# Moving two VectorE casts of chunk 4 behind the masks of chunk 3 in a fused attention and FFN kernel

## The chip, the cores and the metric

The kernel runs on one core of a Trainium2 chip. The metric is the device time of one execution in microseconds; lower is better. TensorE (PE in the profile, with its weight loads as PEld), VectorE (DVE), ScalarE (ACT) and GpSimd (POOL) work beside each other, each through its own instructions in order, and SyncE (SP) issues most of the DMAs in order too. An engine that meets an instruction whose inputs aren't ready waits there with all that stands behind it.

## What is computed

Attention over 4 batches of 8 heads, 768 positions, head size 64, where a query sees the first 4 positions (the sinks) and a window of 128 positions back. Its output, 3072 tokens of 512 numbers, goes through a feed-forward layer that takes the largest of three products:

```python
scores = scale * np.matmul(q, k.transpose(0, 1, 3, 2))
keep = is_sink | in_window
scores = np.where(keep, scores, -1000000000.0)
a = np.exp(scores - np.max(scores, axis=-1, keepdims=True))
a = a / (np.sum(a, axis=-1, keepdims=True) + 1e-09)
x = np.matmul(a, v)                    # then (B*S, H*D)
h = np.maximum(np.maximum(x @ w1, x @ w2), x @ w3)
out = h @ w_out
```

## The kernel before

The tokens are cut into 12 chunks of 256, three to a batch, so that chunks 0, 3, 6 and 9 begin a batch and have no sinks to look back to. A chunk's heads go in four pairs, 0 to 3. For each chunk `load` (lines 93 to 110) brings Q, K and V as float32 into `q_raw`, `k_raw` and `v_raw`, two buffers each; `cast_qk` (112 to 119) turns one half (two pairs) of Q or K into bf16 (`q_bf`, `k_bf`) on the engine that is named in the call; and the halves together are turned to have the head dimension on the partitions, into `qT` and `kT`. Chunks 0 to 3 are turned on TensorE (`turn`). From chunk 4 on a transposing DMA does it (`turn_dma`, 177 to 189), one for Q and, up to chunk 5, two for K. All of them are issued by SP.

Then, pair by pair: `score` (314 to 337) multiplies keys by queries into PSUM (line 331), `expo` (392 to 399) takes the exponential on ScalarE into `e_sb` (line 398), `mask` (401 to 406) multiplies `e_sb` by zeros and ones on VectorE (line 406), and `av` (460 to 476) multiplies it by V (line 471). `av` ends in `norm` (478 to 486), which divides on VectorE by the row sums into `x_sb` (lines 481 and 484). When all four pairs of a chunk are normed, `xpose_dma` (501 to 505) turns `x_sb` into `xT` with one more transposing DMA from SP (line 503). The FFN of a chunk reads `xT`: `ffn_h` (511 to 530) is called nine times a chunk, for three weights and three column blocks, with 8 matmuls each (line 524). Its maximum is a ScalarE copy for the first weight (line 536) and a VectorE maximum for the others (line 540). `ffn_y` multiplies by the output weight (line 553).

There is no scheduler: the kernel is written under `manual_schedule`, and the order of the calls from line 639 on is the order of the instructions on each engine. The FFN of one chunk fills TensorE while the attention of the next is prepared. Around the change the FFN of chunk 2 runs beside the attention of chunk 3, and Q, K and V of chunks 4 to 6 are loaded, cast and turned.

Eight PSUM banks are handed on in the order in which they are given back (`bank` and `give`, 57 to 65). `ffn_h(2, 1, 1)` takes the bank that `ffn_h(2, 0, 1)` has used, `ffn_h(2, 0, 2)` that of pair 0's `norm`.

What stands on the queues between lines 810 and 857, where the change lies:

- VectorE: mask of pair 1, then in the kernel before the cast of half 1 of Q of chunk 4 and of half 0 of K of chunk 4, then the masks of pairs 0 and 3, the maximum for `ffn_h(2, 0, 1)`, the norms of pairs 0 and 1, mask of pair 2, norm of pair 3, two more maxima, a cast for chunk 5, and the norm of pair 2, the last of chunk 3.
- TensorE: scores of pairs 1, 2, 0 and 3, three `ffn_h` of chunk 2 (24 matmuls), `av` of pairs 0 and 1, one `ffn_h`, `av` of pair 3, two `ffn_h`, `av` of pair 2, three `ffn_h`, then sinks and scores of chunk 4 and `ffn_y` of chunk 2, and then `ffn_h(3, 0, 0)`, the first that reads `xT` of chunk 3.
- SP: `turn_dma` of Q of chunk 4, `turn_dma` of its K (two transfers), the load of V of chunk 5 (behind a one-element write of POOL, line 619), `xpose_dma(3)`, the loads of K, V and Q of chunk 6.
- POOL: casts of V of chunk 3 and K of chunk 4, two casts of V of chunk 4, the one-element write, `sink_k` (line 283, two small copies), and from the landing of V of chunk 5 on an unbroken row of casts.

Of the kernel before, what the change touches and what calls it, by code (L numbers as in the profile page):

```python
# [16 lines left out]
def kernel(  # L17
# [13 lines left out]
    nc = tc.nc  # L31
# [17 lines left out]
    with tc.manual_schedule():  # L49
# [7 lines left out]
        def bank(shape, dtype, name):  # L57
            j = free.pop(0)
            x = psum.tile(shape, dtype, tag=f"b{j}", name=name)
            home[id(x)] = x, j  # L60
            return x
# [18 lines left out]
        def keys(ci):  # L80

            return (kT[ci % RING].rearrange("q n p i r -> q (n p i r)")
                    .rearrange("q (p n h c) -> q p n h c", p=NP, n=2, h=2))
# [28 lines left out]
        def cast_qk(ci, w, g, eng):  # L112

            if (ci, w) not in bfs:
                bfs[ci, w] = raw.tile([128, NP, 2, 2, D], BF16, tag=w + "_bf", name=w + "_bf")
            x, y = bfs[ci, w], raws[ci, w]
            f = eng.copy if eng is nc.scalar else eng.tensor_copy
            f(x[:, 2 * g:2 * g + 2].rearrange("q p i a d -> q p a i d"),  # L118
              y[:, 4 * g:4 * g + 4].rearrange("q (p a) i d -> q p a i d", a=2))

        def cast_v(ci, n, i, eng):
            if ci < NEW:
                eng.tensor_copy(  # L123
                    vb[ci % RING][64 * i:64 * i + 64, n, :, 0:D],
                    raws[ci, "v"][64 * n:64 * n + 64, :, i])
                return
            for h in range(2):
                x, y = 64 * h + 32 * i, 64 * n + 32 * h
                eng.tensor_copy(  # L129
                    vb[ci % RING][x:x + 32, n, :, 0:D], raws[ci, "v"][y:y + 32, :, i])  # L130
# [46 lines left out]
        def turn_dma(ci, w):  # L177
            if ci >= NCH:
                return
            if w == "k" and ci < NEW:  # L180
                for n in range(2):
                    nc.sync.dma_start_transpose(
                        out=kT[ci % RING][:, n].rearrange("q p i r -> q (p i) r"),
                        in_=bfs[ci, w][64 * n:64 * n + 64].rearrange("q p i a d -> q (p i a d)"))
                return
            dst = (qT[ci % RING].rearrange("q p i n r -> q (p i) (n r)") if w == "q" else
                   keys(ci).rearrange("q p n h c -> q (p n) (h c)"))
            nc.sync.dma_start_transpose(
                out=dst, in_=bfs[ci, w].rearrange("s p i a d -> s (p i a d)"))
# [124 lines left out]
        def score(ci, pairs):  # L314
            if ci >= NEW:
                return score4(ci, pairs)
            b, c = divmod(ci, CPB)
            kc, qc = kT[ci % RING], qT[ci % RING]
            lo = 0 if c else 1
            for p in pairs:  # L320
                add = (ci, p) in sts
                if not add:
                    sts[ci, p] = [bank([128, 4, 128], F32, "st") for a in range(2)]
                st = sts[ci, p]
                for s, x, n, q0, q1 in ((0, kT[(ci - 1) % RING], 1, 0, 1), (1, kc, 0, 0, 2),
                                        (3, kc, 1, 1, 2)):
                    if s < lo:
                        continue
                    for a in range(2):
                        hp = slice(64 * a, 64 * a + 64)  # L330
                        nc.tensor.matmul(  # L331
                            st[a][:, s:s + q1 - q0].rearrange("q n (i r) -> q n i r", i=2),
                            lhsT=x[hp, n, p].rearrange("q i r -> q (i r)"),
                            rhs=qc[hp, p, :, q0:q1].rearrange("q i n r -> q n i r"),
                            start=not add, stop=True, skip_group_check=add)
                e = work.tile([128, 2, 4, 128], BF16, tag="e", bufs=2 * NP, name="e_sb")
                es[ci, p] = e, st
# [39 lines left out]
        def mask4(ci, p):  # L377
            e = es[ci, p][0]
            if ci % CPB == 0:
                nc.vector.tensor_mul(e[:, :, 1:], e[:, :, 1:], msk0[1])  # L380
                return
            x = work.tile([128, 2, 4, 128], BF16, tag="e", bufs=2 * NP, name="e_sb")


            y = e.rearrange("q a (t j) r -> q (a t) (j r)", t=2)
            (ps, pn), (gs, gn), (cs, cn) = y.ap
            y = bass.AP(tensor=y.tensor, offset=y.offset,
                        ap=[[ps, pn], [gs, gn], [64 * cs, 2], [cs, 128]])
            nc.vector.tensor_mul(x.rearrange("q a (t s) c -> q (a t) s c", t=2), y, msk2)  # L389
            es[ci, p] = x, None  # L390

        def expo(ci, p):
            if ci >= NEW:
                return expo4(ci, p)
            lo = 0 if ci % CPB else 1
            e, st = es[ci, p]
            for a in range(2):
                nc.scalar.activation(e[:, a, lo:], st[a][:, lo:], AF.Exp, scale=scale)  # L398
                give(st[a])

        def mask(ci, p, eng=None):
            if ci >= NEW:
                return mask4(ci, p)
            lo = 0 if ci % CPB else 1
            e = es[ci, p][0]
            (eng or nc.vector).tensor_mul(e[:, :, lo:], e[:, :, lo:], msk0[0] if lo else msk)  # L406
# [104 lines left out]
        def ffn_h(ci, fp, wi, cuts=1, eng=nc.scalar, then=True):  # L511
            if ci not in hs:
                hs[ci] = work.tile([128, FB, 256], BF16, tag="h", bufs=3, name="h_sb")
            hp = bank([128, 2, 256], F32, "h_ps")
            for f in range(2):
                c0 = (2 * fp + f) * 128
                for ds in range(DS):
                    x = xTs[ci][:, ds]
                    if ci < NEW:
                        x = x.rearrange("q t (i r) -> q i t r", i=2)  # L520
                    else:
                        x = (x.rearrange("q t c -> q (t c)")
                             .rearrange("q (j i r) -> q i j r", i=2, r=32))
                    nc.tensor.matmul(  # L524
                        hp[:, f].rearrange("q (i t r) -> q i t r", i=2, r=x.shape[3]),
                        lhsT=w_sb[wi][:, ds, c0:c0 + 128], rhs=x,
                        start=(ds == 0), stop=(ds == DS - 1))
            maxima[ci, fp, wi] = hp
            if then:
                ffn_max(ci, fp, wi, cuts, eng)  # L530

        def ffn_max(ci, fp, wi, cuts=1, eng=nc.scalar):
            hp = maxima.pop((ci, fp, wi))
            dst = hs[ci][:, 2 * fp:2 * fp + 2]
            if wi == 0:
                (nc.scalar.copy if eng is nc.scalar else eng.tensor_copy)(dst, hp)  # L536
            else:
                for f in range(cuts):
                    x = slice(2 * f // cuts, 2 * (f + 1) // cuts)
                    nc.vector.tensor_max(dst[:, x], dst[:, x], hp[:, x])  # L540
            give(hp)
# [273 lines left out]
        cast_v(3, 1, 1, nc.gpsimd)  # L815
        score(3, (0,))
        expo(3, 0)
        cast_qk(4, 'q', 1, nc.vector)
        turn_dma(4, 'q')
        score(3, (3,))  # L820
        cast_qk(4, 'k', 0, nc.vector)
        cast_v(3, 1, 0, nc.gpsimd)
        expo(3, 3)
        mask(3, 0)
        ffn_h(2, 0, 0)
        mask(3, 3)
        ffn_h(2, 1, 0)
        ffn_h(2, 0, 1)
        av_open(3)
# [171 lines left out]
```

## Time and profile before

| | us |
|---|---|
| median of 3 runs | 176.84 (176.4 to 177.53) |
| the profiled execution | 176.56 |
| its span, first to last instruction | 174.8 |
| TensorE busy in it | 168.0 |
| VectorE busy | 126.9 |
| GpSimd busy | 113.1 |
| ScalarE busy | 87.8 |

The profile is of one execution. Times in its rows count from the start of the span. A row of the timeline holds the start, the duration, the engine, the line of the kernel, the operation and what it writes and reads (partitions by elements), how many like it were merged, and in brackets how long the engine sat idle before it and what ended that. SPq is the issue of a DMA by SP, not the transfer: the time from the start of the issue to the landing of the data stands in the view of the DMA issues. The PE clock that was granted is full in every slice of the page.

### The profile page before, as it was taken

The numbers are of one execution on the slowest core, as the hardware profiler recorded it, in microseconds if no ns is written. First come the engines' busy times: TensorE is split into PE (matmuls) and PEld (weight loads), VectorE is DVE, ScalarE is ACT, GpSimd is POOL, SyncE is SP. The second block draws the span as 40 slices with busy tenths as digits, with TensorE's granted clock in tenths as the row PEclk, the third lists the DMA queues.
The fourth block names the chain that finished last, engine by engine and source line by source line (L and its number), as shares of the span: only waits on it lengthen the run. The fifth ranks groups of instructions, "written<-read, shape, count | busy, mean of one in ns | idle before, by whom it ended". The sixth has DMA issues, their size and how long they took to land.

```text
span 174.8 us, 5427 instructions
## 1 busy us (share of the span) xinstructions
PE 168.0 (96%) x2229; PEld 129.4 (74%) x2229; DVE 126.9 (73%) x263; ACT 87.8 (50%) x182; POOL 113.1 (65%) x195
## 2 busy tenths in 40 slices
PE   7988999999989999999999999999999999999992
PEld 2445989756877688697797797797797796896871
DVE  2397665578799768886996886976887776776451
ACT  3688636666852742925827617717636516510210
POOL 6489880076962999999999999999999900000000
PEclk9999999999999999999999999999999999999999
DMA  4999999999977992899999989999999119117303
GB/s 144 292 288 197 237 263 204 270 274 290 285 138 173 200 284 42 192 294 227 247 204 256 270 172 223 267 181 216 244 213 265 32 25 358 44 32 268 124 2 120
DMA packets 70201, 35.22 MB, mean 201 GB/s; under 512 B 27552, under 2 KB 68000, under 8 KB 70176
## 3 DMA queue, kind: packets, MB, share of 16 engines
q1 hardware_dynamic: 64160, 30.55, 73.4%
q0 software_dynamic: 5872, 4.20, 14.5%
q8 instruction: 17, 0.28, 0.6%
q10 hardware_dynamic: 144, 0.13, 0.2%
q14 instruction: 8, 0.07, 0.1%
HBM read 25.17 MB, written 6.29 MB: 180 GB/s over the span
## 4 chain that ended last, share of the span: by engine, by line
PE 70%; DMA 15%; POOL 10%; issue 2%; SPq 1%; DVE 0%; POOLq 0%
PE h_ps L524 44%; PE y_ps L577 11%; PE o L471 5%; DMA w<-in_moe_w_dram 4%; DMA q_raw<-in_q_dram 4%; PE y_ps L553 4%; POOL vb L123 4%; DMA k_raw<-in_k_dram 4%; PE st L357 3%; DMA v_raw<-in_v_dram 3%; POOL w L292 2%; PE st L331 1%; POOL q_raw L107 1%; SPq L107 1%; PE o L453 1%
## 5 line engine op out<-in xcount | busy, mean ns | idle before, releaser
L524 PE MATMUL h_ps<-xT,w 128*128 128x256 bf16 x864 | 101.0, 273 | 0.1
L524 PEld LDWEIGHTS <-w 128*128 128x128 bf16 x864 | 82.0, 98 | 10.1 <-issue 0.3
L540 DVE TENSOR_TENSOR h_sb<-h_sb,h_ps 128x512 bf16<-128x512 bf16 (+1 forms) x74 | 49.1, 671 | 22.1 <-PE h_ps L524 20.7
L536 ACT CAST h_sb<-h_ps 128x512 bf16<-128x512 f32 x36 | 21.1, 592 | 46.5 <-PE h_ps L524 45.5
L129 POOL CAST vb<-v_raw 32x512 bf16<-32x512 f32 x48 | 34.6, 721 | 2.3
L90 POOL CAST k_bf<-k_raw 32x512 bf16<-32x512 f32 x48 | 31.6, 658 | 2.2
L398 ACT ACTIVATE e_sb<-st 128x512 bf16<-128x512 f32 (+1 forms) x48 | 23.3, 583 | 2.3 <-PE st L331 2.3
L484 DVE TENSOR_TENSOR x_sb<-o,rc 128x256 bf16<-128x256 f32 x48 | 20.4, 425 | 1.6
L577 PE MATMUL y_ps<-wo,h_sb 64*64 64x512 bf16 (+1 forms) x312 | 21.1, 377 | 0.0
L123 POOL CAST vb<-v_raw 64x512 bf16<-64x512 f32 x19 | 12.2, 645 | 10.5 <-DMA v_raw<-in_v_dram 9.8
L471 PE MATMUL o<-vb,e_sb 128*128 128x65 bf16 x352 | 16.4, 194 | 1.2 <-POOL ks L283 0.6
L471 PEld LDWEIGHTS <-e_sb 128*128 128x128 bf16 x352 | 14.3, 97 | 3.8 <-DVE e_sb L406 0.9
L389 DVE TENSOR_TENSOR e_sb<-e_part,msk 128x1024 bf16<-128x1024 bf16 x16 | 12.9, 815 | 3.4 <-ACT e_part L374 3.1
L406 DVE TENSOR_TENSOR e_sb<-e_sb,msk 128x1024 bf16<-128x1024 bf16 (+1 forms) x16 | 13.0, 836 | 2.9 <-ACT e_sb L398 2.9
L577 PEld LDWEIGHTS <-h_sb 64*64 64x64 bf16 (+1 forms) x312 | 9.9, 106 | 5.0
L374 ACT ACTIVATE e_part<-st 128x384 bf16<-128x384 f32 x32 | 13.1, 495 | 0.5 <-PE st L357 0.5
L553 PE MATMUL y_ps<-wo,h_sb 128*128 128x512 bf16 x54 | 12.5, 379 | 0.0
L427 ACT ACTIVATE e_sink<-sk 128x256 bf16<-128x256 f32 x8 | 3.1, 388 | 16.5 <-PE sk L423 16.5
L481 DVE RECIPROCAL rc<-o 128x4 f32<-128x4 f32 x48 | 8.4, 174 | 3.9 <-PE o L471 3.8
L553 PEld LDWEIGHTS <-h_sb 128*128 128x128 bf16 x54 | 5.1, 98 | 5.6 <-DVE h_sb L540 0.5
L118 ACT CAST q_bf<-q_raw 128x512 bf16<-128x512 f32 x14 | 8.2, 622 | 0.0
L331 PE MATMUL st<-qT,kT 64*128 64x128 bf16 (+1 forms) x128 | 7.3, 238 | 0.6 <-ACT qT L168 0.5
(91 smaller groups left out, 145.3 us busy)
## 6 DMA issues: line engine op xcount, KB each, us to landing
k_raw<-in_k_dram SPq DMA_DIRECT2D x11, 512.0 KB, 5.5
v_raw<-in_v_dram SPq DMA_DIRECT2D x11, 512.0 KB, 5.6
q_raw<-in_q_dram SPq DMA_DIRECT2D x10, 512.0 KB, 6.7
out_dram<-y_sb SPq DMA_DIRECT2D x8, 512.0 KB, 3.2
w<-in_moe_w_dram POOLq DMA_DIRECT2D x9, 256.0 KB, 6.3
out_dram<-y_sb SPq DMA_DIRECT2D x7, 256.0 KB, 3.4
wo<-in_moe_w_out_dram POOLq DMA_DIRECT2D x2, 384.0 KB, 9.3
q_raw<-in_q_dram SPq DMA_DIRECT2D x2, 256.0 KB, 3.9
```

The source lines that it names most:

```text
L90: f(bfs[ci, "k"][x:x + 32, :, n], raws[ci, "k"][y:y + 32, :, i].rearrange("q (p a) d -> q p a d", a=2))
L123: eng.tensor_copy(vb[ci % RING][64 * i:64 * i + 64, n, :, 0:D], raws[ci, "v"][64 * n:64 * n + 64, :, i])
L129: eng.tensor_copy(vb[ci % RING][x:x + 32, n, :, 0:D], raws[ci, "v"][y:y + 32, :, i])
L374: nc.scalar.activation(dst, st[a], AF.Exp, scale=scale)
L398: nc.scalar.activation(e[:, a, lo:], st[a][:, lo:], AF.Exp, scale=scale)
L471: nc.tensor.matmul(o[:, t, a], lhsT=e[:, a, s], rhs=vb[cv % RING][:, n, 2 * p + a], start=first, stop=True, skip_group_check=True)
L484: nc.vector.tensor_mul(xs[ci][:, p], o[:, :, :, 0:D], rc.unsqueeze(3).to_broadcast([128, 2, 2, D]))
L524: nc.tensor.matmul(hp[:, f].rearrange("q (i t r) -> q i t r", i=2, r=x.shape[3]), lhsT=w_sb[wi][:, ds, c0:c0 + 128], rhs=x, start=(ds == 0 ...
L536: (nc.scalar.copy if eng is nc.scalar else eng.tensor_copy)(dst, hp)
L540: nc.vector.tensor_max(dst[:, x], dst[:, x], hp[:, x])
L553: nc.tensor.matmul(yp, lhsT=hs[ci][:, fb, t * 128:(t + 1) * 128], rhs=wo[:, fb], start=(fb == 0), stop=(fb == FB - 1))
L577: nc.tensor.matmul(yps[ci][t][c:c + cols], lhsT=hs[ci][hp, fb, x:x + cols], rhs=wo[hp, fb], start=(turn == 0 and fb == 0), stop=(turn == 1 ...
```

## The change

The two casts and the turning transfer are called after the masks of pairs 0 and 3 in place of before them; nothing else is altered.

```diff
         score(3, (0,))
         expo(3, 0)
-        cast_qk(4, 'q', 1, nc.vector)
-        turn_dma(4, 'q')
         score(3, (3,))
-        cast_qk(4, 'k', 0, nc.vector)
         cast_v(3, 1, 0, nc.gpsimd)
         expo(3, 3)
         mask(3, 0)
         ffn_h(2, 0, 0)
         mask(3, 3)
+        cast_qk(4, 'q', 1, nc.vector)
+        turn_dma(4, 'q')
+        cast_qk(4, 'k', 0, nc.vector)
         ffn_h(2, 1, 0)
```

On VectorE the rows between the last copy of `xT` of chunk 2 and the first norm of chunk 3 come to stand so (a leading + is new there, a - is gone; `msk_0` is the mask of a chunk that begins a batch; the bracket names the engines or DMA semaphores that the row waits for):

```order
 L498 COPY xT<-xt 128x4x128 [waits PE_49]
 L406 TENSOR_TENSOR e_sb<-e_sb,msk_0_101 128x2x384 [waits Activation_49,Pool_49]
+L406 TENSOR_TENSOR e_sb<-e_sb,msk_0_101 128x2x384 [waits Activation_49] x2
 L118 CAST q_bf<-q_raw 128x2x2x2x64 [waits DMAHW3_49]
 L118 CAST k_bf<-k_raw 128x2x2x2x64 [waits DMAHW5_49]
-L406 TENSOR_TENSOR e_sb<-e_sb,msk_0_101 128x2x384 [waits Activation_49] x2
 L540 TENSOR_TENSOR h_sb<-h_sb,h_ps 128x512 [waits PE_49,Activation_49]
 L481 RECIPROCAL rc<-o 128x4 [waits PE_49]
```

The masks of pairs 0 and 3 have come two instructions forward and the casts two back; what follows them on VectorE is as before.

SP's instructions stand in the same order before and after. These are the ones from the turning of Q of chunk 4 on (`q_bf_867` is that Q, `k_bf_961` its K, `v_raw_1071` V of chunk 5, `x_sb_1011` the attention output of chunk 3, `k_raw_1107` K of chunk 6):

```order
L188 DMA_TRANSPOSE qT0_73<-q_bf_867 128x8x128 [waits DVE_49,PE_49]
L182 DMA_TRANSPOSE kT0_69<-k_bf_961 128x8x64 [waits DVE_49,Pool_49]
L182 DMA_TRANSPOSE kT0_69<-k_bf_961 128x8x64 [waits DMAHW3_49,PE_49]
L107 DMA v_raw_1071<-in_v_dram 128x8x128 [waits DMAHW4_49,Pool_49]
L503 DMA_TRANSPOSE xT_1083<-x_sb_1011 128x8x128 [waits DMAHW5_49,DVE_49,PE_49]
L107 DMA k_raw_1107<-in_k_dram 128x8x128 [waits DMAHW6_49]
```

The first row waits for the moved cast of Q on VectorE, and every row below it is issued after it. TensorE, ScalarE and GpSimd have the same rows in the same order in both kernels.

## The prediction

> **What bounds the kernel now.** First the page, then the chain that ended last.
>
> ```profile
> PE 168.0 (96%) x2229; PEld 129.4 (74%) x2229; DVE 126.9 (73%) x263; ACT 87.8 (50%) x182; POOL 113.1 (65%) x195
> ```
>
> ```profile
> 48.86 0.44 POOL ks L283
> 49.30 0.53 PE o L471 x12
> ...
> 58.96 0.55 PE st L331 x12
> 59.51 1.85 PE h_ps L524 x16
> ...
> 171.45 0.42 DVE y_sb L601
> ```
>
> TensorE is busy for 96% of the span, and from 49.30 us on the chain is TensorE's work alone up to the last copy. So whatever TensorE loses after 49 us, the kernel loses, and a stall removed is a gain only if no other takes its place. The waits between 44 and 62 us show which are near:
>
> ```profile
> PEld L471 <- DVE e_sb L406: 0.9, 1, 0.9
> PE o L471 <- POOL ks L283: 0.6, 1, 0.6
> PEld L524 <- DMA xT<-x_sb: 0.2, 1, 0.2
> ```
>
> And the timeline of that stretch:
>
> ```profile
> 45.34 2.40 ACT L398 ACTIVATE e_sb<-st 128x384 bf16<-128x384 f32 x6
> ...
> 45.88 2.78 PE L524 MATMUL h_ps<-xT,w 128*128 128x256 bf16 x24
> ...
> 46.31 0.94 DVE L406 TENSOR_TENSOR e_sb<-e_sb,msk 128x768 bf16<-128x768 bf16 x1 [0.88 <-ACT e_sb L398]
> 46.91 1.57 POOL L123 CAST vb<-v_raw 64x512 bf16<-64x512 f32 x2
> 47.18 0.83 DVE L118 CAST q_bf<-q_raw 128x512 bf16<-128x512 f32 x1
> ...
> 47.93 0.83 DVE L118 CAST k_bf<-k_raw 128x512 bf16<-128x512 f32 x1
> 48.09 1.33 SPq L188 DMA_TRANSPOSE qT<-q_bf  x1
> ...
> 48.56 0.73 POOL L283 COPY ks<-kT 64x16 bf16<-64x16 bf16 x2
> 48.68 1.02 DVE L406 TENSOR_TENSOR e_sb<-e_sb,msk 128x768 bf16<-128x768 bf16 x2
> ...
> 49.28 0.54 PE L471 MATMUL o<-vb,e_sb 128*128 128x65 bf16 x12 [0.62 <-POOL ks L283]
> 49.51 2.54 SPq L182 DMA_TRANSPOSE kT<-k_bf  x2
> 49.63 0.68 DVE L540 TENSOR_TENSOR h_sb<-h_sb,h_ps 128x512 bf16<-128x512 bf16 x1
> ...
> 52.15 0.54 SPq L107 DMA_DIRECT2D v_raw<-in_v_dram  x1
> ...
> 53.84 0.42 DVE L118 CAST q_bf<-q_raw 128x512 bf16<-128x512 f32 x1
> ...
> 54.38 0.42 DVE L484 TENSOR_TENSOR x_sb<-o,rc 128x256 bf16<-128x256 f32 x1
> ...
> 54.87 1.23 SPq L503 DMA_TRANSPOSE xT<-x_sb  x1
> ...
> 55.65 0.61 PE L331 MATMUL st<-qT,kT 64*128 64x128 bf16 x12
> ```
>
> Two places matter. At 48.66 (45.88 + 2.78) TensorE has ended its three `ffn_h` and idles for 0.62 us until the first `av` of chunk 3 at 49.28. The profile puts that on POOL's small copies, but `av` doesn't read `ks`; the weight load beside it waits for the mask of pair 0, which starts on VectorE at 48.68, behind both casts. The two masks take 1.02 together, so the first ends near 49.2, and 49.28 follows. Its input was ready at about 47.0: the six exponentials of 45.34 to 47.74 start some 0.38 apart, and pair 0's are the third and fourth. So the casts cause the stall.
>
> The second place is 59.44, ten microseconds on:
>
> ```profile
> 59.44 0.66 PEld L524 LDWEIGHTS <-w 128*128 128x128 bf16 x7 [0.16 <-DMA xT<-x_sb]
> ```
>
> There the FFN of chunk 3 begins, and its first weight load waited for the turned attention output. TensorE lost nothing, since the scores before it ran until then (58.96 + 0.55), but the transfer has no slack: TensorE can't pass this point sooner unless `xT` lands sooner, and is later by whatever `xT` is late.
>
> **The change, part by part.** Nothing is added or removed: two masks go forward, two casts and what hangs on them go back.
>
> *The stall.* The mask of pair 0 takes the place of the cast of Q at 47.18. Nothing shows it there; its bounds are 0.51 (half of 1.02) and the 0.94 that the mask at 46.31 took while POOL was casting. Even by the latter it ends at 48.12, before 48.66. The mask of pair 3 ends by 49.1 and is needed after 12 `av` and 8 FFN matmuls, near 49.9. The 0.62 goes; taken alone, −0.62.
>
> *When the cast of Q ends.* Before, at 48.01 (47.18 + 0.83). After, behind two masks. If the second mask runs in the clear, it ends no earlier than 48.5 (47.18 + 0.87, the distance of the first two rows of VectorE, + 0.47), and a cast in the clear (0.42, the row at 53.84) near 48.9. If mask and cast are both slow, 47.18 + 0.87 + 0.87 + 0.83 = 49.75. I take 49.4: the cast that began at 47.93 ended 0.28 after POOL's second cast (48.48), 0.14 less than a cast in the clear takes, as if it had had to wait for POOL first and then run. A mask that does so ends 0.37 after POOL's cast, and POOL's cast, itself held by a longer VectorE instruction, ends near 48.6. So the mask ends at 48.97, the cast about 0.35 later, and a little is lost to the small copies of POOL. The Q cast ends 1.4 later, between 0.9 and 1.75.
>
> The Trainium skill, "SBUF — State Buffer", section "Who interferes with whom", says that a VectorE instruction with two SBUF inputs and a GpSimd instruction that reads SBUF exclude each other for the whole instruction, and that issue order decides who blocks. The pairs of rows above agree with it (0.94 against 0.51, 0.83 against 0.42). If the two instead shared at half speed, the second mask would end near 48.75, the cast at 49.1, and the sum below would come to +0.5 and not +0.8.
>
> *SP.* It turns Q at 48.09, the two halves of K at 49.51 and loads V of chunk 5 at 52.15, each issue within 0.1 of the end of the one before. So they all move by 1.4: to about 49.5, 50.9 and 53.55. The turning of `xT` at 54.87 follows the norm that ends at 54.80 (54.38 + 0.42), not SP. VectorE leaves the moved piece at about 49.75 instead of 49.63, and is without a pause up to that norm, so `xT` is issued near 55.0 (between 54.5 and 55.4).
>
> *What the transfers do to each other.* Issue to landing, of V of chunk 5, of `xT` of chunk 3, and of all nine `xT`:
>
> ```profile
> v_raw<-in_v_dram SPq DMA_DIRECT2D x1, 512.0 KB, 4.2
> ```
>
> ```profile
> xT<-x_sb SPq DMA_TRANSPOSE x1, 4.5
> ```
>
> ```profile
> xT<-x_sb SPq DMA_TRANSPOSE x9, 3.1
> ```
>
> V lands at 56.35 (52.15 + 4.2), `xT` at 59.37 (54.87 + 4.5). After the change V lands at 57.75. Is `xT` held by it? The nearest case is the next turning, of Q of chunk 5, issued behind the load of Q of chunk 6:
>
> ```profile
> 57.45 1.64 SPq L107 DMA_DIRECT2D q_raw<-in_q_dram  x1
> 59.18 3.52 SPq L188 DMA_TRANSPOSE qT<-q_bf  x1
> ```
>
> ```profile
> q_raw<-in_q_dram SPq DMA_DIRECT2D x1, 512.0 KB, 7.3
> qT<-q_bf SPq DMA_TRANSPOSE x1, 6.5
> ```
>
> The load landed at 64.75, the turning at 65.68, 0.93 behind it: transfers of this queue end in order. So `xT` comes between 0.93 behind V (58.7) and 3.0 behind it (60.75; 3.0 is its distance before, which has some pause in it). Which is nearer? Its 4.5 are 1.4 longer than the median. The DMA view from 55.9 to 59.4, in 40 slices of 0.09 us, shows why:
>
> ```profile
> GB/s 0 23 132 222 214 219 208 219 205 202 225 369 205 167 129 138 144 118 123 64 18 6 15 9 15 9 12 9 9 9 9 199 339 310 345 158 117 304 293 293
> q8 instruction: 1, 0.02, 1.6%
> ```
>
> At some 200 GB/s the bulk is through in about 1.5 us; then for 1 us only some 9 GB/s flow, as if one DMA engine of 16 had its share left. The one packet of instructions that fell there took 1.6% of 16 engines in 3.5 us, or 0.9 us of one engine. That engine has V's share, the packet and `xT`'s share to move, in any order, so it isn't done before 57.75 + 1.5 + 0.9 = 60.15. I take that: `xT` lands 0.8 later than before, between −0.65 and +1.4.
>
> *Sum.* TensorE comes to 59.44 up to 0.62 earlier, less what VectorE holds up between, waits for `xT` there, and goes on 0.8 later than before. The removed 0.62 is inside that wait. 176.56 + 0.8 = 177.36 against the profiled execution. The median of the runs lies 0.28 above that execution, so a median after would be near 177.6; I name 177.5.
>
> *What costs nothing, and why.* The keys of chunk 4 land at about 50.8 + 2.8 = 53.6 before and 55.0 after; the first score that reads them is at 55.65, at the earliest 55.03 after the change. If they are late, TensorE waits there and not at `xT`. The landing and the need of the step that POOL's delay of 1.4 reaches first, the turned keys of chunk 6, stand far enough apart (74.09 + 4.1 = 78.2 against 81.71):
>
> ```profile
> kT<-k_bf SPq DMA_TRANSPOSE x2, 2.8
> ```
>
> ```profile
> 74.09 1.35 SPq L188 DMA_TRANSPOSE kT<-k_bf  x1
> ```
>
> ```profile
> kT<-k_bf SPq DMA_TRANSPOSE x1, 4.1
> ```
>
> ```profile
> 81.71 0.52 PE L357 MATMUL st<-qT,kT 64*64 64x256 bf16 x16
> ```
>
> **The rivals.** *The stall goes and `xT` isn't late.* If the instruction packet falls elsewhere, or `xT` gets past V, it lands at 58.7 to 59.3. TensorE then keeps 0.1 to 0.62 of the gain: 175.9 to 176.5. For it: with the packet out, 57.75 + 1.5 is 59.25. Against: the packet comes where TensorE's instructions run out, which this change shifts by half a microsecond at most, and V and `xT` together keep the engines busy around it. It decides if V lands before about 57.0, that is if the cast of Q ends by 48.65.
>
> *Both ends go wrong.* The cast of Q waits for POOL's small copies too (49.75), V lands at 58.1, and `xT` keeps its full 3.0 behind V, at 61.1: +1.7, 178.3 by the profiled execution, 178.6 by the median. For it: 3.0 is the only distance measured for this pair. Against: part of it was a pause between V's last and `xT`'s first data.
>
> *That the masks don't come earlier* can't be: their inputs are ready at 47.0 and 47.8.
>
> **How the numbers follow.** The forecast (`xT` late by 0.3 to 1.4, 176.9 to 178.2): 0.62. The first rival: 0.2. The second, with anything worse: 0.18. The range goes from the middle of the first rival to the second's price: 176.2 to 178.7. One per cent, about what a measurement of this kernel can tell from no change, is 1.77 us, so the bounds are 175.07 and 178.61 against the median of 176.84. The whole forecast lies within, and so does the first rival; only the second reaches over the upper one: faster 0.03, same 0.78, slower 0.19.
>
> **What would show it.** Right: no idle before the `av` at 48.7; the masks at 47.2 and 48.05 with some 0.9 each; the turning of Q issued near 49.5, V's load near 53.55, V landing near 57.75; a wait of TensorE of 1 us or more for `xT` ahead of the first FFN matmul of chunk 3, which starts near 60.2; everything after that shifted by the same amount. Wrong: `xT` landing before 59.4 while V lands at 57.7 or later, TensorE stopped by VectorE instead (the maximum whose bank `ffn_h(2, 1, 1)` takes over), or a new wait after 60 us.

## The result and the profile after

| | before | after |
|---|---|---|
| median of 22 runs each, us | 176.72 | 177.69 |
| ratio of the two, 95% interval | | 1.0051 (1.0037 to 1.0066) |
| the profiled execution | 176.56 | 177.44 |
| its span | 174.8 | 175.7 |

The change costs 0.9 us (0.0051 of 176.7); the ratio is that of the means, without one slow run after (179.96, granted clock 0.99), and the medians differ by 0.97. The first line of the page after shows no engine busier than before by more than 0.4 us:

```profile
PE 168.4 (96%) x2224; PEld 129.7 (74%) x2229; DVE 125.9 (72%) x263; ACT 87.9 (50%) x182; POOL 111.3 (63%) x195
```

In the chain that ended last (start, duration, what), a transfer now stands between two stretches of TensorE work, where the kernel before had none after 49.30:

```profile
46.51 2.78 PE h_ps L524 x24
...
52.64 1.92 PE h_ps L524 x18
54.56 5.76 DMA xT<-x_sb
60.37 1.92 PE h_ps L524 x16
...
171.04 1.32 PE y_ps L599 x12
```

The waits of 44 to 63 us after (total, count, longest) say the same. The wait of `av` (line 471), 0.6 on TensorE before, is no longer in the list, and there is a wait of 1.0 that was not there:

```profile
PEld L524 <- DMA xT<-x_sb: 1.2, 1, 1.2
...
PE h_ps L524 <- DMA xT<-x_sb: 1.0, 1, 1.0
```

The timeline after shows each step between:

```profile
46.51 2.78 PE L524 MATMUL h_ps<-xT,w 128*128 128x256 bf16 x24
46.66 1.50 POOL L123 CAST vb<-v_raw 64x512 bf16<-64x512 f32 x2
46.94 2.09 DVE L406 TENSOR_TENSOR e_sb<-e_sb,msk 128x768 bf16<-128x768 bf16 x3 [0.88 <-ACT e_sb L398]
...
48.96 0.42 DVE L118 CAST q_bf<-q_raw 128x512 bf16<-128x512 f32 x1
...
49.13 0.53 PE L471 MATMUL o<-vb,e_sb 128*128 128x65 bf16 x12
...
49.45 1.33 SPq L188 DMA_TRANSPOSE qT<-q_bf  x1
...
53.52 0.53 SPq L107 DMA_DIRECT2D v_raw<-in_v_dram  x1
...
54.56 1.55 SPq L503 DMA_TRANSPOSE xT<-x_sb  x1
...
60.37 1.81 PE L524 MATMUL h_ps<-xT,w 128*128 128x256 bf16 x15 [1.02 <-DMA xT<-x_sb]
```

The three masks run one behind the other, and `av` follows the 24 matmuls without a pause: the stall is gone. The cast of Q ends at 49.38 (48.01 before), so SP turns Q at 49.45 (48.09) and loads V of chunk 5 at 53.52 (52.15). `xT` is issued at 54.56, a little sooner than before (54.87), and lands later. The views of the DMA issues of V and of `xT`, from issue to landing:

```profile
v_raw<-in_v_dram SPq DMA_DIRECT2D x1, 512.0 KB, 4.4
```

```profile
xT<-x_sb SPq DMA_TRANSPOSE x1, 5.8
```

V lands at 57.92 (56.35 before) and `xT` at 60.36 (59.37): the FFN of chunk 3 starts at 60.37 in place of 59.44. That is 0.93, the whole difference between the two spans. From there to the end of the span it is 115.3 us after and 115.4 before.

One thing in this execution is not the change's: TensorE was already 0.63 late at 46.51 (45.88 before), from a slower start (the 12 warm-up matmuls alone took 5.30, 4.76 before). A second execution, below, settles that.

### The profile page after: what moved, and what is told of

Its sections match the earlier page's. It is cut to its first block, busy times and chain, and to the rows that moved or that the text cites. A ratio compares the mean times of both kernels' runs of the same rounds, so it can differ in the third digit from the quotient of the medians.

```text
span 175.7 us, 5422 instructions
## 1 busy us (share of the span) xinstructions
PE 168.4 (96%) x2224; PEld 129.7 (74%) x2229; DVE 125.9 (72%) x263; ACT 87.9 (50%) x182; POOL 111.3 (63%) x195
## 4 chain that ended last, share of the span: by engine, by line
PE 91%; DMA 3%; DVE 2%; ACT 1%; issue 1%
PE h_ps L524 54%; PE y_ps L577 10%; PE o L471 6%; PE y_ps L553 5%; DMA xT<-x_sb 3%; PE st L357 3%; PE warm L203 3%; PE st L331 2%; PE pt L138 2%; PE st L311 1%; PE o L453 1%; DVE vb L123 1%; PE y_ps L599 1%; PE sk L423 1%; PE xt L496 1%
```

## The experiments

The theory (A): the time is set by the landing of `xT` of chunk 3, and `xT` is late for two reasons together, V of chunk 5, which the later turning of Q pushes back in SP's order, and the packet of 16 KB of TensorE's instructions that is fetched while `xT` is under way. The rivals: V alone is the cause; the packet alone; or the loss is an accident of the execution that was profiled.

All versions with an unchanged start (and those with 112 more instructions, which kept it) stand in one table. Landing is the issue's start plus the time from issue to landing; the start of `ffn_h` of chunk 2 shows how late an execution was ahead of the change; the last but one column is the span less the start of the first FFN matmul of chunk 3.

| version | `ffn_h` of chunk 2 | V5 lands | `xT` issued | `xT` lands | FFN of chunk 3 starts | span less that | ratio to before (95%) |
|---|---|---|---|---|---|---|---|
| before | 45.88 | 56.35 | 54.87 | 59.37 | 59.44 | 115.4 | 1 |
| after | 46.51 | 57.92 | 54.56 | 60.36 | 60.37 | 115.3 | 1.0051 (1.0037 to 1.0066) |
| e12, after once more | 46.20 | 58.46 | 55.03 | 60.83 | 60.87 | 115.4 | 1.0051 (1.002 to 1.0083) |
| e1, V behind `xT` | 46.04 | 61.51 | 54.78 | 59.68 | 59.73 | 116.7 | 1.0083 (1.0063 to 1.0104) |
| e2, V ahead of Q | 46.13 | 52.03 | 55.06 | 59.46 | 59.49 | 115.4 | 0.9993 (0.9976 to 1.001) |
| e3, before, V ahead | 46.15 | 52.66 | 55.53 | 60.03 | 60.13 | 115.4 | 1.0016 (1.0 to 1.0031) |
| e4, only K's cast moved | 46.15 | 56.71 | 54.67 | 59.57 | 59.64 | 115.4 | 0.9993 (0.9978 to 1.0008) |
| e6, after, packet moved | 45.85 | 58.62 | 54.66 | 59.46 | 59.54 | 115.4 | 1.0005 (0.9991 to 1.0018) |
| e9, before, packet moved | 45.84 | 57.23 | 54.24 | 58.34 | 59.12 | 115.4 | 0.9991 (0.9972 to 1.001) |
| e10, e4, packet moved | 46.01 | 57.55 | 54.52 | 59.32 | 59.33 | 115.4 | 0.9977 (0.996 to 0.9994) |
| e11, e2, packet moved | 46.00 | 51.84 | 54.89 | 58.09 | 59.58 | 115.4 | 1.0017 (0.9999 to 1.0035) |

In all but e1 the rest of the kernel takes 115.3 to 115.4 us from that one matmul on. Whatever a version does ahead of it counts only by when it starts.

### e12: the changed kernel once more

No edit.

> The changed kernel once more, nothing edited, for a second profiled execution. In the first, the three ffn_h of chunk 2 began at 46.51, 0.63 later than in the kernel before, with nothing changed ahead of that place; in the other versions with an uncut warm-up they began at 46.04 to 46.15. From the start of the first ffn_h matmul of chunk 3 to the end of the span it is 115.3 to 115.5 us in those versions. Theory A (the loss belongs to the change): with a start near 46.1 the load of V of chunk 5 lands near 57.5, the instruction packet still falls on the turning of xT, xT lands 2 to 3 behind V, the first ffn_h matmul of chunk 3 starts at 59.9 to 60.5 after a wait for xT of 0.6 to 1.2, and the median is 177.4 to 178.0, some 0.9 above the kernel before. Rival B (the first execution showed 0.63 of an accidental late start and only 0.3 of the change): the start is near 46.0, xT lands at 59.5 to 59.8, the wait is under 0.5, and the profiled execution comes to 176.7 to 177.0.

Measured: median 177.9 (before beside it 176.8). The timeline of the second execution:

```profile
46.20 2.78 PE L524 MATMUL h_ps<-xT,w 128*128 128x256 bf16 x24
46.63 2.44 DVE L406 TENSOR_TENSOR e_sb<-e_sb,msk 128x768 bf16<-128x768 bf16 x3 [0.88 <-ACT e_sb L398]
...
47.84 1.71 POOL L123 CAST vb<-v_raw 64x512 bf16<-64x512 f32 x2
...
48.99 0.83 DVE L118 CAST q_bf<-q_raw 128x512 bf16<-128x512 f32 x1
...
50.81 1.91 PE L524 MATMUL h_ps<-xT,w 128*128 128x256 bf16 x16 [0.41 <-DVE h_sb L540]
...
60.87 1.38 PE L524 MATMUL h_ps<-xT,w 128*128 128x256 bf16 x11 [1.28 <-DMA xT<-x_sb]
```

It began half as late and ended later. The cast of Q met a cast of POOL this time and took 0.83, because POOL was later: it cast an earlier V, for whose load it waits, at 43.48, against 42.52 in the first execution. V of chunk 5 landed at 58.46, `xT` 2.37 behind it, and TensorE waited 1.28. So the loss belongs to the change. The start was above the expected 59.9 to 60.5, since V landed 1 us later than expected. The row at 50.81 shows a second thing: of the stall that was removed, 0.41 came back at once, as a wait of `ffn_h(2, 1, 1)` for the VectorE maximum that frees its bank. The DMA view of 55.5 to 61.5 in 40 slices of 0.15 us:

```profile
GB/s 89 130 31 58 212 259 256 345 348 348 348 350 333 301 294 259 143 44 333 268 270 195 10 0 0 7 9 9 10 10 10 307 348 147 246 297 294 283 290 297
...
q8 instruction: 1, 0.02, 1.1%
```

For nine slices, 58.8 to 60.15, no more than 10 GB/s flow. The packet (the line of q8: 1.1% of 16 engines in 6 us, or 1.06 us of one) starts at about 58.25, with `xT` under way. Of the 35 data packets that start in these nine slices 30 are under 512 bytes, as those of a turning are (all 447 from 56.0 to 56.6 in e1, when only `xT` moves), and those of a load are not (none of 510 from 55.9 to 56.7 in after). So it looks like a last share of `xT` on one engine, with the loads behind it standing too.

### e1: V behind xT

```diff
-        load(5, 'v', gate=pool_gate)
         av(3, 2)
         xpose_dma(3)
+        load(5, 'v', gate=pool_gate)
```

> The changed kernel with one move: V of chunk 5 is loaded behind the turning of xT of chunk 3 instead of ahead of it. Theory one (the queue: xT lands 2.4 us behind V, and V is late because the turning of Q is): xT has nothing ahead of it, lands some 3.1 us after its issue near 54.6, or 4.1 with the instruction packet on one engine, so at 57.7 to 58.7, and TensorE doesn't wait for it at 59.4 less. The stall that the change removed stays removed: 0.5 to 0.6 below the kernel before, near 176.1. V lands some 2 us later still, which POOL has to carry. Theory two (VectorE and the delayed casts hold the chain, whatever is in the queue; or POOL's later casts of V of chunk 5 do): no better than the changed kernel, 177.6, or worse by POOL's further 2 us.

Measured: 178.15 (before beside it 176.76); theory one had 176.1 and missed, and the time lies where theory two put it, between 177.6 and 2 us more for POOL. The two stops of TensorE:

```profile
59.73 1.92 PE L524 MATMUL h_ps<-xT,w 128*128 128x256 bf16 x16 [0.47 <-DMA xT<-x_sb]
```

```profile
70.73 0.45 PE L331 MATMUL st<-qT,kT 64*128 64x128 bf16 x8 [1.17 <-DMA kT<-k_bf]
```

The FFN of chunk 3 started 0.64 and 1.14 sooner than in the two executions of the changed kernel. What the move gave, it took back with more at the scores of chunk 5: POOL had waited 8.4 us for V, and the keys of chunk 5 were cast and turned later. But `xT` still took 4.9 us with no load ahead of it in the queue, so V is not all of it. The DMA view of 55.5 to 60.5 (slices of 0.125 us) shows why:

```profile
GB/s 0 0 0 33 166 205 199 205 166 188 6 0 0 0 0 0 0 0 6 8 8 10 10 10 125 289 283 287 324 332 336 287 303 307 291 287 299 287 303 287
...
q8 instruction: 1, 0.02, 1.4%
```

`xT` flows at some 200 GB/s until 56.75, then hardly moves for 14 slices, 1.75 us, and the rest comes from 58.5 on. For 1.0 us almost nothing starts, about the time of the packet (1.4% of 16 engines in 5 us, or 1.1 us of one); from 57.75 to 58.5 only 26 small data packets follow, at 6 to 10 GB/s, as if one engine of 16 made up its share while the others waited for it. With no load ahead of it, the one packet holds up the transfer as a whole, and for longer than it takes itself.

### e2 and e3: V ahead of the turning of Q, with and without the change

```diff
         cast_v(3, 1, 1, nc.gpsimd)
+        cast_v(3, 1, 0, nc.gpsimd)
+        load(5, 'v', gate=pool_gate)
         score(3, (0,))
```

The two calls are gone from their old places; e3 makes the same move in the kernel before.

> The changed kernel with V of chunk 5 loaded ahead of the turning of Q of chunk 4, as soon as POOL has cast V of chunk 3. Theory one: V is out of the way by about 52, the turned Q and K land up to 1 us later than in the changed kernel (53 to 55.5, the first score needs them at 55.5), xT lands by 58.7, and TensorE doesn't wait for it: near 176.1, 0.6 below before. Theory two (VectorE): still 177.6. If the turned keys come late, a new wait of 0.3 to 1 us stands at the first score of chunk 4 and the time is 176.4 to 177.1.

> The kernel before (casts ahead of the masks) with V of chunk 5 loaded ahead of the turning of Q of chunk 4. xT lands sooner, but TensorE still loses 0.6 at the first av of chunk 3, since the mask of pair 0 is still behind the casts. Theory one: the same as before within 0.2, 176.7, with 0.6 of idle near 48.7 and none for xT; the difference between this and the same with the casts moved is the worth of the removed stall, 0.6. A rival in which the order of the transfers alone is worth something gives less than 176.4.

Measured: e2 176.76, e3 177.01 (before beside them 176.76). With V landed at 52.03 the changed kernel is back at the time of before, but not below it, where theory one expected 176.1. In e2 the wait for `xT` is gone from TensorE, and its stop at 50.78 is the one that e12 has at 50.81:

```profile
50.78 1.91 PE L524 MATMUL h_ps<-xT,w 128*128 128x256 bf16 x16 [0.44 <-DVE h_sb L540]
...
59.49 1.92 PE L524 MATMUL h_ps<-xT,w 128*128 128x256 bf16 x16
```

e3 was a miss in its size: 0.3 slower than expected. In its profile POOL's two casts of V ran from 48.03 to 49.47 (46.91 to 48.48 before) and met the masks (two in 1.42, 1.02 before), so the stall was 1.01 and not 0.6. The one-element write that now stands ahead of them took 0.09; most of the delay is older than the edit, since POOL cast an earlier V at 43.69 (42.77 before), as late as in e12, where nothing was edited:

```profile
49.94 0.54 PE L471 MATMUL o<-vb,e_sb 128*128 128x65 bf16 x12 [1.01 <-DVE e_sb L406]
```

Between e3 and e2 only the change differs: with V out of the way it is worth 0.25 us (177.01 against 176.76), with a stall of 1.0 removed; the intervals of the two in the table overlap, so even this isn't clear of noise.

### e4: only K's cast moved

```diff
         score(3, (3,))
-        cast_qk(4, 'k', 0, nc.vector)
...
         mask(3, 3)
+        cast_qk(4, 'k', 0, nc.vector)
```

The kernel before, with the cast of Q and its turning left in their place.

> The kernel before with the cast of K alone moved behind the masks of pairs 0 and 3; Q's cast and its turning stay ahead. The turning of Q is issued as before, so V and xT are where they were. Theory one: the mask of pair 0 starts some 0.75 earlier (47.9 instead of 48.7), may run slow beside POOL, and the stall of 0.62 falls to between 0 and 0.2; but xT lands as before at 59.4, so TensorE waits there instead: 176.7, the same as before. Theory two (only the stall and the work on VectorE count): 0.4 to 0.6 faster, 176.1 to 176.3.

Measured: 176.61 (before beside it 176.76). SP's turning of Q stays at 48.20, V lands at 56.71. Half the edit takes most of the stall away, and the rest goes into the wait for `xT`:

```profile
49.06 0.54 PE L471 MATMUL o<-vb,e_sb 128*128 128x65 bf16 x12
...
59.64 1.92 PE L524 MATMUL h_ps<-xT,w 128*128 128x256 bf16 x16 [0.36 <-DMA xT<-x_sb]
```

TensorE idles 0.13 at the first (46.15 + 2.78 = 48.93), where it idled 0.62 before. The loss of the change is thus in the move of Q, which is what stands ahead of V on SP; and a stall removed without touching V brings nothing either, because `xT` lands when it did.

### e5, e7, e8: the packet moved by 176 more instructions

To move the packet, the 12 warm-up matmuls at the start (their product is never read) were cut into 100 narrower ones of nearly the same total width (6100 columns for 6144): 176 TensorE instructions more (a matmul and a weight load each). The page's line of q8 counts 17 packets and 0.28 MB in both kernels and 18 packets and 0.29 MB in these versions and the next four, which is how the packets, of some 16 KB each, are known to hold TensorE's instructions. e5 does so to the kernel after, e7 to before, e8 to e4.

```diff
-                    nc.tensor.matmul(pw, lhsT=wz[:, 0:128], rhs=wz, start=True, stop=True)
+                    nc.tensor.matmul(pw[:, 0:61], lhsT=wz[:, 0:128], rhs=wz[:, 0:61], start=True, stop=True)
...
-        warm(8)
+        warm(67)
...
-        warm(4)
+        warm(33)
```

> The changed kernel with the 12 warm-up matmuls of 512 columns at the start cut into 100 of 61 columns: the same columns in all, 176 TensorE instructions more, so that the packet of instructions that was fetched at 58.2 us is fetched at another time (some 80 instructions later in the program, behind the first FFN matmul of chunk 3). The warm-up's result is used by nothing. Theory one (the packet holds one DMA engine for 1 us while it has its share of xT to move): xT of chunk 3 lands 4.8 us after its issue instead of 5.8, TensorE's wait for it falls from 1.0 to 0.2 or less, 0.7 to 0.9 less, 176.8 to 177.0. Rival (V ahead of it in the queue is the whole delay, the packet is beside the point): 5.8 as before and 177.6 within 0.2.

> The kernel before with the warm-up cut into 100 matmuls: what the cut and the moved packets do by themselves. xT of chunk 3 lands 3.2 to 3.5 us after its issue instead of 4.5, but TensorE loses its 0.62 at the first av as before and comes to the FFN of chunk 3 at the same time: 176.7 within 0.2 by both theories. If it is slower by more, the cut warm-up costs at the start, and the other runs are read against this one.

> The kernel with the cast of K alone moved, and the warm-up cut into 100 matmuls. There the stall at the first av is down to 0.13, and a wait of 0.36 for xT took its place. Theory one: with the packet out of the way xT lands about 1 us sooner, the wait is gone, and the removed stall is worth 0.3 to 0.5 at last: 176.2 to 176.4. Rival: 176.6, as without the cut.

Measured: 178.35, 178.34 and 178.22 (before beside them 176.77). All three missed, for a reason that has nothing to do with the question: the `ffn_h` of chunk 2 began at 47.94, 47.26 and 47.28, so the start of the kernel had lost 1.1 to 1.4 us against the versions that they were made from. Only distances inside an execution can be read: without the packet near it, `xT` landed 0.96 (e5) and 1.26 (e8) behind V, where it had been 2.44 and 2.86; in e7 it was 1.58, from 3.02.

### e6, e9, e10, e11: the packet moved by 112 more instructions

The same with 90 columns, `warm(45)` and `warm(23)`, made to after (e6), before (e9), e4 (e10) and e2 (e11). This start is not disturbed (45.84 to 46.01).

> The same with 68 warm-up matmuls of 90 columns, 112 instructions more: the packet comes 112 instructions sooner, near 53 us, when the queue is waiting for the turnings of K to be issued and an engine that is held has time to catch up. Theory one: as in the run with 176 more, 176.8 to 177.0. If the engine doesn't catch up, V and xT are still late on it: 177.2 to 177.6. Rival: 177.6.

> The kernel before with the warm-up cut into 68 matmuls, the control of the run that did this to the changed kernel. There the start was as in the kernel before (the warm-up took 4.73 us), the packet came at 51.7, and the change cost nothing (1.0005). Theory one: xT lands sooner here as well, but the 0.62 at the first av stays, so 176.7 within 0.2, and the changed kernel with the cut is not slower than this one. Rival (the cut warm-up by itself makes any of these kernels faster by 0.8): 175.9.

> The cast of K alone moved, with the warm-up cut into 68 matmuls. Theory one: the stall at the first av is 0.1 to 0.2, the wait of 0.36 for xT is gone since no packet falls on xT, and 0.3 to 0.5 are gained on the kernel before: 176.2 to 176.4. Rival (moving the packet is of no use, the wait for xT stays): 176.6 to 176.7.

> Both casts moved, V of chunk 5 loaded ahead of the turning of Q, and the warm-up cut into 68 matmuls: neither V nor a packet is in the way of xT. TensorE still loses some 0.4 to VectorE, the maximum whose bank ffn_h(2, 1, 1) takes over, so it comes to the FFN of chunk 3 at 59.2 to 59.5. Theory one: 176.5 to 176.8, no better than before: the removed stall is given back to VectorE here. Rival (only xT held it): 176.1.

Measured: e6 176.89 (before beside it 176.77); e9 176.73, e10 176.42, e11 177.04 (before beside them 176.62). The rows of e6:

```profile
54.02 0.54 SPq L107 DMA_DIRECT2D v_raw<-in_v_dram  x1
...
59.54 1.92 PE L524 MATMUL h_ps<-xT,w 128*128 128x256 bf16 x16 [0.36 <-DMA xT<-x_sb]
```

V was issued later than in after and landed later (58.62 against 57.92), yet `xT` landed 0.9 sooner, 0.84 behind V. The packet had moved to a place near 52, onto the turnings of K, whose issue took SP 3.47 in place of 2.55, and V is issued behind them; no line of q8 stands in its DMA view of 55.5 to 60.5. Moving the packet alone took 0.8 us off the changed kernel (177.69 to 176.89). The medians and the control e9 carry this figure, not the two traces: the profiled execution of e6 also came to the `ffn_h` of chunk 2 sooner than the two of after, by 0.66 and 0.35. The cleanest pair is e2 and e11, with V out of the way in both. From issue to landing of `xT`, e2 and then e11:

```profile
xT<-x_sb SPq DMA_TRANSPOSE x1, 4.4
```

```profile
xT<-x_sb SPq DMA_TRANSPOSE x1, 3.2
```

So the packet costs a turning 1.2 us here. In e4 and e10 the pair is less clean: 4.9 and 4.8, but V landed 0.84 later in e10, where the packet fell at about 52.1, onto V's load (issued at 52.35). e9 shows that the kernel before doesn't gain from this: `xT` landed at 58.34, 0.8 ahead of need, and the time stayed, since TensorE still came to 59.12 through the stall of `av` (0.34 there; this execution took 176.19, 0.5 less than the median of e9). e10 is the one version that beats both kernels, the one before by 0.23% (0.06 to 0.4): K's cast alone moved, V issued early (52.35), and the packet off `xT`. As one interval of thirteen, and one that ends so near to none, this is weak evidence; and the wait for `xT`, which was expected to go, was still 0.20. e11 was slower than expected (176.5 to 176.8): in its profiled execution TensorE waited 0.29 for the VectorE maximum and its weight load 0.3 for the turned keys, and started the FFN at 59.58 with `xT` there since 58.09.

## Why the prediction was right

*The stall.* "The 0.62 goes" holds in both executions. "The removed 0.62 is inside that wait" holds in the first; in e12 0.41 of it went to the wait for the VectorE maximum, and only the rest into that for `xT`. The prediction took the 0.16 ahead of the first weight load of chunk 3 as the sign that it waits for `xT`; the same 0.16 stands there in e9 and e11, with `xT` landed 0.8 and 1.5 before, and is put down to issue. What does show the missing slack is the landing, 59.37 against a start at 59.44. The masks in the three rows took 0.70 (after) to 0.85 (e1) each, 0.9 was forecast; they ended in time all the same.

*When the cast of Q ends.* The forecast was 1.4 later, between 0.9 and 1.75. Counted from the first mask (2.44, 3.19, 2.89 and 2.67 in after, e12, e1 and e6, 1.70 before) it is 0.74, 1.49, 1.19 and 0.97. The forecast end of 49.4 (49.38 measured) was met in the first execution with 0.63 from its late start in it: the size of this step was near the upper end of what four executions show, so that this part of the agreement is luck, and its lower bound was too high. Between after and e12 the difference is whether the cast meets a cast of POOL: it took 0.42 in after, where POOL was done at 48.16, and 0.83 in e12, where POOL went on to 49.55. There it ended 0.27 behind POOL; at half speed through the 0.56 that they had in common it would have ended 0.14 behind. The Trainium skill, "SBUF — State Buffer", section "Who interferes with whom", has the two engines exclude each other for a whole instruction; a cast that waited and then ran in full would have ended 0.42 behind. The 0.27 lies midway, so no run here decides between the two.

*SP.* Q to V was forecast as 4.05 (49.5 to 53.55) and took 4.07 and 4.06. V then took 4.4 and 4.5 where 4.2 was taken, and landed 1.57 and 2.11 later than before. VectorE didn't hold the issue of `xT` back: 54.56 and 55.03, forecast 55.0.

*xT behind V.* Forecast 2.4 (1.5 of bulk and 0.9 of packet), measured 2.44 and 2.37: the sum was right, its two terms were not. The bulk was through at about 58.8 in e12, 0.34 behind V and not 1.5, and without the packet the whole turning landed 0.84 behind V in e6. The packet cost more than 0.9: with it and without it the distances differ by 1.1 (e4 and e10) to 1.9 (before and e9). That the two errors cancel is luck. The picture behind the terms, one DMA engine that is late while the others finish, fits the end of the turning in e12; e1, where the packet came in the middle, shows the whole turning held up. The distances fall in two groups: 2.37 to 3.02 where the packet falls on `xT` (before, after, e12, e4), 0.84 to 1.77 where it doesn't (e5 to e10). Most of the "3.0 behind V" of the kernel before was thus the packet and not the load, and the bounds of 0.93 and 3.0 were near the two cases.

*The sum.* Forecast +0.8, measured +0.9, by way of a start of the FFN at 60.37 and 60.87 (forecast 60.2) and a wait of 1.02 and 1.28 (forecast 1 or more).

*The rivals.* That `xT` isn't late was nearly made true twice, by V (e2) and by the packet (e6): it landed at 59.46 in both (58.7 to 59.3 in the rival), and the times were 176.76 and 176.89 where the prediction had 175.9 to 176.5. In e11 it was wholly true (58.09), and the time was 177.04. Here the rival was too hopeful. The mechanism was right (either cause taken away ends the loss), but the gain of 0.1 to 0.62 never came, because the next waits stood close behind: the bank that VectorE frees (0.44 in e2) and the rest of the wait for `xT` (0.36 in e6). That both ends go wrong (V at 58.1, `xT` 3.0 behind) came true by half in e12, V at 58.46 but `xT` 2.37 behind it. The stop by VectorE's maximum, which the prediction named as a sign against itself, came in e12 too (0.41), but ahead of the wait for `xT`, which covered it.

What stays open: why `xT` landed as late as it did in the first execution of after, whose DMA view shows the packet but no full stop like that of e12 and e1. Its data had all started to move by 58.35 (of the 345 data packets from there to 59.05 none is under 512 bytes), and the landing came 2.0 later; in e6 it came 0.5 after the last such packet. That the packet, which starts at about 58.2 and takes 1.0, held the landing back is likely and not shown. Open too is why e7 and e10 kept 1.58 and 1.77 without a packet near, and whether e11 is slower than before at all (0.17%, from none to 0.35%); its profiled execution, at 176.66, is level with the 176.62 of before. Why the start differs by up to 0.63 between executions wasn't tried.

## What to carry to other kernels

A stall on the busiest engine is worth only the distance to the next wait on that engine: before removing one, look for the next place where a DMA lands just in time (here `xT` landed 0.07 ahead of its first use), because the stall may be slack that it needs. When a cast is moved back, follow the DMA that it feeds down its queue: everything issued in order behind it moves too, and here the one that hurt was a load three places on, ahead of the transfer on the path. When one place sets the end, read each version by the start of the instruction there; the remainder was the same to 0.1 us in ten executions of nine versions.

## What was not expected of the hardware

A single packet of some 16 KB of instructions all but stopped a transposing DMA that was under way for 1.35 and 1.75 us (at most 10 GB/s in e12 and e1; the first execution of after shows no such stop), though the packet itself takes 1.1 us of one engine, and cost it 1.2 us from issue to landing (4.4 in e2, 3.2 in e11). Where it falls depends on how many instructions TensorE was given before: 112 more at the start, whose result nothing reads, took 0.8 us off the changed kernel and nothing that can be measured off the kernel before (0.9991). Finer cutting has its own price at the start: 100 matmuls of 61 columns in place of 12 of 512 left the kernel 1.1 to 1.4 us behind at 46 us, 68 of 90 columns did not.
